# One core's adaLN block: dense column products, two detours through PSUM, and a new order of all operations

## The chip, the cores and the metric

The kernel runs on one NeuronCore of one Trainium2 chip. A core has five engines that run side by side, each through its own queue in order: TensorE (PE, matrix products; its weight loads are shown as PEld), VectorE (DVE), ScalarE (ACT), GpSimd (POOL) and SyncE (SP), which here only issues DMA transfers. Products are written to PSUM, eight banks of 2 KB in each of 128 partitions; everything else lies in SBUF. [...] The metric is device microseconds of one execution.

## What is computed

A transformer block on x of 2048 rows and 512 columns, all in fp32. Six modulation vectors come from one condition vector c. The first half is a linear attention with 32 heads of 16, the second a gated MLP that mixes over the rows:

```python
mod = (silu(c) @ w_mod).reshape(c.shape[0], 6, 1, -1)
sa, ca, ga, sb, cb, gb = (mod[:, k] for k in range(6))
h = layernorm(x) * (1 + ca) + sa
x = x + ga * A(h, wqkv, wo)
h = layernorm(x) * (1 + cb) + sb
x = x + gb * B(h, w_in, w_sp, b_sp, w_out)

# A: linear attention
phi = lambda t: where(t > 0, t + 1, exp(t)) + 1e-6
pq, pk = phi(q), phi(k)
kv  = einsum("bhsd,bhse->bhde", pk, v);  z = einsum("bhsd->bhd", pk)
num = einsum("bhqd,bhde->bhqe", pq, kv)
den = einsum("bhqd,bhd->bhq", pq, z)[..., None] + 1e-6
out = (num / den) merged over heads, @ wo

# B: gated MLP over rows
z = gelu(x @ w_in);  z1, z2 = halves;  z2 = layernorm(z2)
g = einsum("ts,bsf->btf", w_sp, z2) + b_sp[None, :, None]
out = einsum("bsf,fd->bsd", z1 * g, w_out)
```

## The kernel before

The 2048 rows are 16 tiles of 128, numbered t. Nearly every product is done in three passes on pairs of rounded and remaining parts (`mm3`, L108): hi x hi, hi x lo, lo x hi. Each operand is therefore split first: ACT makes the rounded part, DVE or POOL the difference.

The work runs in these stages.

*Start.* The column products `col_mm` (L191) multiply w_mod's second block with silu(c) and give 1 + ca as one column per 128 features. Its weights are 128x128 pieces of w_mod, the moving operand is one column of `sil`, the output one PSUM column. `col_end` (L206) copies the four columns to SBUF. `mean_col` (L325) spreads each of them over 128 columns, four ACT operations from the constant tile `inv` (all 1/512). `mean_mm` (L330) multiplies that with the raw key and query weights to get the mean over features of the scaled weights; `w_mid` (L336) then folds scale and mean into the weights, and `w_hi`, `w_lo` split them. Between the column products stand dummy products (`dummy`, L172; "du" in the order), whose results are not used.

*Projections and moments.* For each tile the x tile is loaded twice, once already transposed (`load_xt`). `k_mm` and `q_mm` give keys and queries in two PSUM banks in turn ("pso"). `phi_in` or `phi_raw` with `phi_add` scale and shift them. `phi_exp` (L438) then makes relu(-t + tiny) and its exponential on ACT, both in one SBUF tile, and `phi_end` (L443) adds max(t, tiny) to it on DVE. `g_mm` accumulates the moments of phi(k) with the normalised x over all 16 tiles.

*Second stage.* The moments are multiplied with the value weights and with wo; the queries are divided by their denominators (`den1`, `den2`), transposed by DMA, and multiplied (`wo_mm`); `x1_out` adds to x, stores it and takes its statistics; `h2` calls `ln_apply` (L259), two DVE operations that scale and shift, both in one SBUF tile; the result is transposed by DMA, split, and multiplied with w_in (`z_mm`), and gelu and the layer norm of its second half follow.

*Row mixing and output* (from ORDER3 on). The first four row tiles of w_sp times z2 are done plainly ("pp"), the rest by a two-by-two scheme with seven products ("pr"). The result is multiplied by z1, transposed by DMA, split and multiplied with w_out ("wm").

Order. Nothing is scheduled by the framework. Two strings, ORDER (from ORDER on, run by `run_all`) and ORDER3, list every operation by a two-letter name and its arguments; each engine receives its instructions in that order. Relevant names: "cm" column product, "ce" col_end, "mc" mean_col, "mr" mean_mm, "wf"/"qh"/"qd"/"qg" fold and split the weights, "kk", "km", "qm" key and query products, "k2"/"q2" phi_exp, "k4"/"q4" phi_end, "h2", "g1"/"g2" gelu of z's two halves, "l5" the load of the sixth modulation block, "lk", "ly", "lw", "lm", "lx" loads. SLOTS lists for each pool which of its buffers every new tile takes, in the order of the list; a tile must wait until the last user of its buffer is done. PSUM's pool "t" (`ps("t", ...)`, "pst") has two banks; the column products, mean products, biases, broadcasts and PE's transposes take them, 17 times in all. Loads and stores are all issued by SP.

Of the kernel before, what the change touches and what calls it, by code (L numbers as in the profile page):

```python
# [26 lines left out]
def block_kernel(ctx: ExitStack, tc: tile.TileContext, x, x_t, w_qkv, w_o, w_in, w_sp, b_sp, w_out,  # L27
# [163 lines left out]
    def col_mm(m, kc):  # L191
        if m not in CP:
            CP[m] = ps("t", [P, KC], f"pcol{m}")
        for i in range(KC):
# [1 line left out]
            mm(CP[m][:, i:i + 1], RAW["mod", m, kc // 2][:, kc % 2, i * P:(i + 1) * P], sil[:, kc:kc + 1],
               start=n == 1, stop=n == KC * KC, skip_group_check=True)
# [61 lines left out]
    def ln_apply(key, src, scale, shift, name):  # L259
        h = sb("ta", [P, D], F32, name)  # L260
        nc.vector.scalar_tensor_tensor(h, src, MEAN[key], scale, op0=OP.subtract, op1=OP.mult)  # L261
# [906 lines left out]
```

## Time and profile before

| | us |
|---|---|
| median of 3 runs | 656.33 (650.57 to 656.46) |
| the profiled execution | 656.31 |
| its span, from first to last instruction | 654.2 |
| bytes moved | 105.74 MB, mean 162 GB/s |

The page gives busy times of each engine over the span, a table in 40 slices, the chain of work that ended last, and groups of instructions by line and shape. Matmuls are pipelined and their ends are modelled, so PE's busy time overstates how densely it works; the distance between the starts of products is the finer measure. A line such as L444 is a line of the kernel; a tile name stands for all tiles of that name with their numbers left out. The rows on which the argument rests are shown in the prediction.

### The profile page before, as it was taken

The page shows a single profiled execution, that of the slowest core. Times are in us where ns is not written, and L with a number is a line of the kernel's source. Part 1 is how long each engine was busy: PE and PEld are TensorE (multiplying, and loading weights), DVE is VectorE, ACT ScalarE, POOL GpSimd, SP SyncE. Part 2 cuts the span into 40 slices and gives each one's busy share as a digit, 9 for nine tenths or more (in the row PEclk, how much of TensorE's full clock was granted, in tenths as well). Part 3 has the DMA queues.
Part 4 walks back from the last instruction along what each step waited for, and adds up shares of the span by engine and source line. Part 5 has one row for each costly group of instructions (what it writes and reads, how often), then busy time and mean ns, then how long its engine had stood idle before and what let it go on. Part 6 is the DMA issues. An engine that isn't in the chain of part 4 may idle for free.

```text
span 654.2 us, 9565 instructions
## 1 busy us (share of the span) xinstructions
PE 629.8 (96%) x3407; PEld 568.7 (87%) x3407; DVE 506.2 (77%) x910; ACT 334.6 (51%) x563; POOL 226.6 (35%) x186
## 2 busy tenths in 40 slices
PE   9999989999889899979999999999999999999998
PEld 9587777777778889879899999999999999998886
DVE  0789999998779689864884579799698789884762
ACT  1577775646446865457452564445444345443430
POOL 0562425625674566633524521140312221110000
PEclk9999999999999999989999999999999999999999
DMA  8235431344234555863473586642745767689862
GB/s 285 105 111 176 129 96 34 113 124 142 61 110 121 116 135 143 199 156 100 142 228 124 174 314 235 150 146 85 215 99 169 209 173 223 173 314 251 261 233 89
DMA packets 91310, 105.74 MB, mean 162 GB/s; under 512 B 57120, under 2 KB 57632, under 8 KB 91264
## 3 DMA queue, kind: packets, MB, share of 16 engines
q1 hardware_dynamic: 91264, 105.15, 53.5%
q8 instruction: 26, 0.43, 0.3%
q14 instruction: 20, 0.16, 0.1%
HBM read 66.07 MB, written 25.95 MB: 141 GB/s over the span
## 4 chain that ended last, share of the span: by engine, by line
PE 44%; DVE 15%; ACT 7%; issue 4%; DMA 3%; POOL 2%; SPq 0%; DVEq 0%; ACTq 0%; POOLq 0%
PE P L930 18%; PE Pq L930 9%; PE z L652 3%; PE pout L111 3%; PE pout L112 3%; PE pout L110 3%; DVE xpp L279 2%; DVE bst L250 2%; DVE xph L279 1%; POOL mv L255 1%; DVE h L262 1%; DMA wor<-in_w_out 1%; DVE ht L299 1%; DVE xr L628 1%; DVE h L261 1%
## 5 line engine op out<-in xcount | busy, mean ns | idle before, releaser
L652 PE MATMUL z<-win,ht 128*128 128x344 f32 x768 | 126.8, 324 | 7.3 <-DVE ht L299 2.8
L652 PEld LDWEIGHTS z<-win,ht 128*128 128x128 f32 x768 | 122.5, 191 | 11.4 <-DVE ht L299 3.5
L930 PE MATMUL P<-z,f 128*128 128x344 f32 x576 | 95.4, 320 | 1.1 <-DVE f L920 1.0
L930 PEld LDWEIGHTS P<-z,f 128*128 128x128 f32 x576 | 91.3, 188 | 1.7 <-DVE f L920 1.6
L920 POOL TENSOR_TENSOR f<-raw_wsp,f 128x512 fp32r<-128x512 f32 x24 | 37.5, 1575 | 122.9 <-ACT f L917 98.6
L255 POOL TENSOR_TENSOR mv<-ve,mhalf 128x1 f32<-128x1 f32 x48 | 37.5, 798 | 74.5 <-DVE ve L254 57.6
L930 PE MATMUL Pq<-z,wsp 128*128 128x344 f32 x384 | 61.5, 321 | 1.3 <-ACT mod L241 1.3
L930 PEld LDWEIGHTS Pq<-z,wsp 128*128 128x128 f32 x384 | 61.0, 188 | 1.6 <-ACT mod L241 1.5
L917 ACT ACTIVATE f<-sa 128x512 fp32r<-128x512 f32 x36 | 22.7, 630 | 50.2 <-DVE sa L907 12.5
L917 ACT ACTIVATE f<-raw_wsp 128x512 fp32r<-128x512 f32 x48 | 29.1, 625 | 21.4 <-PE P L930 9.4
L688 POOL TENSOR_TENSOR z<-zz,z 128x688 fp32r<-128x688 f32 x16 | 29.1, 1834 | 26.0 <-ACT z L685 26.0
L920 DVE TENSOR_TENSOR f<-sa,f 128x512 fp32r<-128x512 f32 x36 | 27.2, 758 | 9.1 <-ACT f L917 9.0
L111 PE MATMUL pout<-wout,ut 128*128 128x512 f32 (+1 forms) x85 | 32.5, 382 | 0.3 <-DVE wout L1050 0.3
L112 PE MATMUL pout<-wout,ut 128*128 128x512 f32 (+1 forms) x85 | 32.3, 380 | 0.0
L110 PE MATMUL pout<-wout,ut 128*128 128x512 f32 (+1 forms) x85 | 32.2, 379 | 0.0
L269 ACT COPY uca<-us 128x768 uint16<-128x768 uint16 x32 | 25.0, 828 | 13.8 <-DVE us L985 10.3
L472 POOL TENSOR_TENSOR pksum<-pksum,tk 128x512 f32<-128x512 f32 x15 | 22.7, 1511 | 26.3 <-DVE tk L444 19.5
L110 PE MATMUL kp<-wk,ht 128*128 128x512 f32 x64 | 26.0, 407 | 3.2 <-DVE tk L423 3.2
L1019 ACT ACTIVATE ut<-ur 128x384 fp32r<-128x384 f32 x32 | 15.5, 519 | 26.4 <-DMA ur<-ud 11.5
L269 ACT COPY xph<-h 128x512 uint16<-128x512 uint16 x28 | 15.9, 615 | 22.4 <-DVE h L262 17.8
L111 PE MATMUL kp<-wk,ht 128*128 128x512 f32 x64 | 25.4, 397 | 1.0 <-DVE wk L345 1.0
L112 PE MATMUL po<-m,pt 128*128 128x512 f32 x64 | 25.3, 396 | 0.6 <-POOL pt L299 0.6
(257 smaller groups left out, 1553.6 us busy)
## 6 DMA issues: line engine op xcount, KB each, us to landing
raw_wsp<-in_w_sp SPq DMA_DIRECT2D x32, 512.0 KB, 5.0
ud<-uca SPq DMA_DIRECT2D x16, 384.0 KB, 3.7
ur<-ud SPq DMA_DIRECT2D x16, 384.0 KB, 4.9
z1d<-z SPq DMA_DIRECT2D x16, 344.0 KB, 2.4
zd<-zz SPq DMA_DIRECT2D x16, 344.0 KB, 2.8
z1r<-z1d SPq DMA_DIRECT2D x16, 344.0 KB, 3.7
xt<-in_x_t SPq DMA_DIRECT2D x16, 256.0 KB, 2.8
x<-in_x SPq DMA_DIRECT2D x16, 256.0 KB, 2.8
```

What stands on the lines that cost most here:

```text
L110: mm(o, a_hi, b_hi, start=first, stop=False, **kw)
L111: mm(o, a_hi, b_lo, start=False, stop=False, **kw)
L112: mm(o, a_lo, b_hi, start=False, stop=last, **kw)
L255: nc.gpsimd.tensor_tensor(mv[:, 1:2], ve, mhalf, op=OP.pow)
L269: nc.scalar.copy(pl[:, h], v[:, :, h])
L279: copy(o[:, :, h], plt[:, h * n:(h + 1) * n].rearrange("p a b -> p (a b)"))
L472: nc.gpsimd.tensor_add(pksum, pksum, PK[t])
L652: mm(p[:, b, :HB], a[:, i, kc], win[h][:, j, kc, b * HB:(b + 1) * HB], start=kc == 0 and k == 0, stop=kc == KC - 1 and k == 2)
L688: nc.gpsimd.tensor_sub(Z2[t][:, 1], ZZ[t], f(Z2[t][:, 0]))
L917: nc.scalar.activation(SF[p, h, k][:, 0], s_src(p, h, k), AF.Copy)
L920: eng.tensor_sub(SF[p, h, k][:, 1], s_src(p, h, k), f(SF[p, h, k][:, 0]))
L930: mm(B[key][:, :HB], a[:, x_], b[:, y_], start=i == 1, stop=i == n)
```

## The change

1. `col_mm` writes 128 equal columns for each feature block: the moving operand is silu(c)'s column broadcast to 128 columns, the output a whole PSUM bank of 4 x 128 columns. `col_end` reads the first column of each block for this key.
2. `mean_col` becomes one ACT operation from that bank, (p + 1)/512, which no longer needs `col_end` or `inv`; the tile `inv` and its fill go.
3. `ln_apply` puts the first of its two results into a PSUM bank of pool "t" and reads it from there.
4. `phi_exp` keeps only the relu; the exponential moves into `phi_end` and writes to a PSUM bank of pool "t", from which DVE's sum reads. Pool "t" is now taken 65 times.
5. ORDER and ORDER3 list the operations in a new order, and SLOTS has new buffers to fit. Six of eleven dummy groups are left out of ORDER: four stand before the first column product and one before the first mean product. The operations of ORDER3 are the same as before, in another order.

```diff
-        "md": "0312013210121201201020120122021201020",
+        "md": "032130213313212312213212313231321312",
...
-        "pst": "01010101010110101",
+        "pst": "01010101010101010101010101010101010101010101010101010101010101010",
...
-    inv = sb("md", [P, P], F32R, "inv")
-    nc.gpsimd.memset(f(inv), 1.0 / D)
...
     def col_mm(m, kc):
         if m not in CP:
-            CP[m] = ps("t", [P, KC], f"pcol{m}")
+            CP[m] = ps("t", [P, KC, P], f"pcol{m}")
         for i in range(KC):
             n = NCOL[m] = NCOL.get(m, 0) + 1
-            mm(CP[m][:, i:i + 1], RAW["mod", m, kc // 2][:, kc % 2, i * P:(i + 1) * P], sil[:, kc:kc + 1],
-               start=n == 1, stop=n == KC * KC, skip_group_check=True)
+            mm(CP[m][:, i], RAW["mod", m, kc // 2][:, kc % 2, i * P:(i + 1) * P],
+               sil[:, kc:kc + 1].to_broadcast([P, P]), start=n == 1, stop=n == KC * KC, skip_group_check=True)
...
     def col_end(key):
         COL[key] = const.tile([P, KC], F32, name=f"col{key}")
-        nc.scalar.activation(COL[key], CP[key], AF.Copy, bias=1.0 if key == 1 else 0.0)
+        p = CP[key][:, :, 0] if key == 1 else CP[key]
+        nc.scalar.activation(COL[key], p, AF.Copy, bias=1.0 if key == 1 else 0.0)
...
     def ln_apply(key, src, scale, shift, name):
         h = sb("ta", [P, D], F32, name)
-        nc.vector.scalar_tensor_tensor(h, src, MEAN[key], scale, op0=OP.subtract, op1=OP.mult)
-        nc.vector.scalar_tensor_tensor(h, h, RSTD[key], shift, op0=OP.mult, op1=OP.add)
+        p = ps("t", [P, D], "p" + name)
+        nc.vector.scalar_tensor_tensor(p, src, MEAN[key], scale, op0=OP.subtract, op1=OP.mult)
+        nc.vector.scalar_tensor_tensor(h, p, RSTD[key], shift, op0=OP.mult, op1=OP.add)
         return h
...
-    def mean_col(kc):
-        if "c" not in WC:
-            WC["c"] = sb("tb", [P, KC, P], F32, "cbr")
-        nc.scalar.activation(WC["c"][:, kc], f(inv), AF.Copy, scale=COL[1][:, kc:kc + 1])
+    def mean_col():
+        WC["c"] = sb("tb", [P, KC, P], F32, "cbr")
+        nc.scalar.activation(WC["c"], CP[1], AF.Copy, scale=1.0 / D, bias=1.0 / D)
...
     def phi_exp(key):
         EK[key] = sb("tb", [P, D], F32, f"e{key[0]}{key[1]}")
         nc.scalar.activation(EK[key], TK[key], AF.Relu, scale=-1.0, bias=tiny)
-        nc.scalar.activation(EK[key], EK[key], AF.Exp, scale=-1.0)
 
     def phi_end(key, o):
-        nc.vector.scalar_tensor_tensor(o, TK.pop(key), TINY, EK.pop(key), op0=OP.max, op1=OP.add)
+        p = ps("t", [P, D], f"p{key[0]}{key[1]}")
+        nc.scalar.activation(p, EK.pop(key), AF.Exp, scale=-1.0)
+        nc.vector.scalar_tensor_tensor(o, TK.pop(key), TINY, p, op0=OP.max, op1=OP.add)
...
     ORDER = """
-        lm1,0 si du1 du2 du3 du4 du5 cm1,0 lm1,1 du6 cm1,1 lm1,2 du7 cm1,2 lm1,3 lk1 lk0 du8 cm1,3 ce1 mc0 ly1
-        mc1 mc3 mc2 lk2 th1 tl1 ly0 th0 tl0 du9 mr1,0 mr1,1 mr1,2 lk3 mr1,3 wf1,3 qh1,3 wf1,1 qh1,1 lw0,0
-        mr0,0 mr0,1 lm0,1 lw0,1 mr0,2 mr0,3 qg1,3 wf1,0 qh1,0 wf1,2 qh1,2 lm0,0 yp0,0 qd1,0 lx0 qg1,1 qd1,2
-        kk0,0 du10 du11 kk0,1 kk1,0 kk0,2 yp0,1 kk0,3 lm0,3 yp0,3 kk1,1 kk1,2 wf0,1 wf0,3 lm0,2 yp0,2 ly2
...
+        lm1,0 lm1,1 si du1 du2 du3 du4 cm1,0 cm1,1 lm1,2 cm1,2 lm1,3 cm1,3 mc lk0 ly1 th1 tl1 lk1 lk2 ly0 th0
+        tl0 lk3 du5 mr1,0 mr1,1 mr1,2 mr1,3 ce1 wf1,3 lw0,0 mr0,0 mr0,1 qh1,3 qg1,3 lw0,1 mr0,2 wf1,0 qh1,0
+        wf1,1 qh1,1 qg1,1 wf1,2 qh1,2 qd1,0 qd1,2 lm0,1 yp0,1 lm0,3 mr0,3 wf0,3 lm0,0 yp0,0 ya0,1 kk1,0 lm0,2
+        yp0,2 ya0,2 wf0,1 yp0,3 ya0,3 wf0,2 wf0,0 ly5 th5 lx0 qh0,1 s10 kk0,0 qh0,3 kk0,1 kk1,1 kk1,2 kk1,3
...
```

More of the change, by code (lines that the diff above doesn't have):

```diff
@@ L810, in block_kernel @@
-        bh15 mS3 bh14 bl14 gm11 bl15 gm12 gm13 qm13 q113 zs zr d12 d13 mB3 d22 vb mB4 wl0,1 d10 d14 gm14 gm15
-        gh0 gh1 li at2 gh2 mk gh3 d11 d23 kv0 l5 lW0,3 wh1,0 d20 kv1 lW0,2 wh0,2 kv2 kv3 kx wh0,3 qm15 wl0,3
-        qm14 d21 wl1,0 q115 lX4 at0 ae0 ae2 mm0 wh1,2 mm1 d17 me0 me1 mm2 me2 mm3 lW1,1 d15 me3 q114 lX0 at3
-        ae3 wh1,1 wl1,1 lW1,3 wl0,2 at1 ae1 wo0 x10 wo3 d24 wo1 x13 w02 h20 ht0 wl1,2 w12 ap4 q213 lX1 d25 he0
-        z00 wh1,3 wl1,3 x12 ap5 am4 ah4 al4 za0 zb0 wo4 h22 hp2 h23 d27 lX11 hp3 am5 ah5 al5 wo5 g10 g20 x11
@@ L815, in block_kernel @@
-        hm2 h21 hh2 hl2 hm3 d16 q413 q214 zl0 ap7 d18 d110 hh3 q414 lX8 ht1 he1 zn0 zp0 d26 z12 g22 zl2 q215
-        z01 lX6 g11 hl3 x14 h24 d19 ap6 hp4 d210 z02 g12 am7 x15 am6 hm4 hh4 h25 z13 g23 ap10 zn2 z11 d112 hl4
-        z04 hp5 z14 q415 d115 d28 g21 ah7 al7 wo7 d29 ah6 al6 g14 zl1 zh2 zl3 d111 d215 hm5 lX7 g24 ap9 am10
-        hh5 wo6 hl5 z15 x17 ap8 zp2 d211 h27 am9 hp7 d212 ah10 g25 al10 zl4 am8 ah8 al8 z03 g13 zn4 zh0 zo0
-        lX10 ah9 zo2 hm7 lX9 z05 hh7 g15 ap11 wo10 wo8 x16 ap12 zl5 hl7 z17 d113 h26 hp6 al9 wo9 x110 lX14 zp4
@@ new lines, in block_kernel @@
+        me2 d14 at3 lW1,3 wh1,3 mm1 me1 at1 q114 mm3 me3 wo0 ae3 wo3 d15 wh1,0 lX4 wl1,0 w02 d24 lW1,1 wh1,1
+        lX0 x10 ae1 wo1 q214 d17 ap4 x13 wl1,1 h20 ht0 d25 he0 w12 za0 z00 wl1,3 x12 zb0 ap5 am4 ah4 al4 wo4
+        q213 h22 hp2 d27 h23 q413 hp3 q215 am5 ah5 al5 wo5 lX9 hm2 lX5 x11 h21 ht1 hh2 hl2 z12 ap7 hm3 g10 x14
+        g20 zl0 he1 q414 hh3 hl3 q415 d115 g22 zn0 z01 g11 x15 h24 hp4 z02 d16 d111 d26 z13 h25 hp5 g12 hm4
+        hh4 ap6 g23 l5 d18 d19 d28 lX8 hl4 hm5 hh5 am7 ah7 al7 z11 g21 zh0 zo0 lX7 hl5 lX6 zl2 z04 d211 z14
@@ new lines, in block_kernel @@
+        g14 am6 ah6 ap8 d110 z03 d29 wo7 g24 zp0 d210 zn2 d215 ap10 zp2 zl4 ap9 al6 x17 d112 g13 zn4 zp4 h27
+        zh2 z15 hp7 z05 am10 ah10 wo6 al10 d113 am8 ah8 am9 wo10 al8 wo8 ap11 d212 zl3 x16 ah9 ap12 al9 wo9
+        h26 hp6 x110 hm7 hh7 x18 hl7 g15 h28 z07 g25 z17 lX12 hp8 am11 ah11 al11 wo11 hm6 hh6 d213 x19 hm8 hh8
+        hl6 z16 hl8 z08 g27 lX11 am12 ah12 g17 h29 hp9 al12 wo12 zh4 zo4 x111 ap13 h211 zn3 zp3 hm9 zl5 h210
+        hh9 hl9 zl7 g18 zo2 d114 hp11 hp10 zh3 g26 zl6 zn5 zp5 lX15 d214 z19 g29 z06 g16 hm10 hh10 ap14 z09
@@ L828, in block_kernel @@
+        zl11 zn11 zh11 zo9 z115 g114 zp11 mB5 aL0,0 aL1,0 g215
     """
@@ L1132, in block_kernel @@
+        wm3 uh4 ot1 ul4 ur6 uh6 um14 up14 ur10 ug12 uq12 uq13 ul6 ur7 ux14 lx14 lz15 wm4 uh5 wm2 ot2 uh8 ur9
+        ul5 ug14 uq14 lx11 uh7 lx6 wm6 ul7 lx10 ot3 ur12 uh10 ur13 ul8 wm5 uh12 wm8 cd7,4 um15 up15 wm7 ot4
+        ot5 ur11 ur14 ul10 uh9 lx13 ul9 ot6 ux15 ot7 ot8 uh14 ul14 wm10 ul12 wm9 wm12 ug15 uq15 uh11 ul11 wm11
+        ot9 ot10 uh13 ul13 wm13 ur15 uh15 wm14 ot11 ot12 ul15 wm15,0,256 ot13 ot14 ot15,0,256 wm15,256,512
+        ot15,256,512
     """
```

162 lines of the change are left out of this document (78 added, 84 removed).

## The prediction

> **What bounds the kernel now.** I read the page's head first, then the table by stages, then who PE waits for, and then the first 28 us line by line.
>
> ```profile
> span 654.2 us, 9565 instructions
> ...
> PE 629.8 (96%) x3407; PEld 568.7 (87%) x3407; DVE 506.2 (77%) x910; ACT 334.6 (51%) x563; POOL 226.6 (35%) x186
> ```
>
> PE is busy for 96% of the span, so only three things can be had: PE work that need not be done, PE work at a low clock, and the 24.4 us in which PE stands idle.
>
> ```profile
> core 0: us, PE busy (x) PEld busy (x) DVE busy (x) ACT busy (x) POOL busy (x), PEclk, DMA share, GB/s
> 0.00:24.40 24.40, 23.41 (x84) 18.44 (x85) 4.58 (x10) 5.92 (x13) 1.93 (x10) 1.00 0.72 258
> 24.40:130.00 105.60, 102.70 (x445) 81.49 (x444) 100.70 (x171) 74.78 (x122) 52.56 (x42) 1.00 0.33 103
> 130.00:300.00 170.00, 156.01 (x825) 137.00 (x824) 138.39 (x254) 96.97 (x164) 93.39 (x80) 0.99 0.48 126
> 300.00:360.00 60.00, 59.12 (x350) 55.98 (x349) 39.05 (x71) 30.98 (x48) 24.00 (x19) 1.00 0.53 162
> 360.00:587.00 227.00, 224.69 (x1421) 223.65 (x1420) 186.35 (x327) 106.98 (x185) 54.76 (x38) 1.00 0.62 191
> 587.00:655.00 68.00, 63.83 (x292) 52.14 (x290) 37.13 (x81) 18.99 (x36) 0.00 (x0) 1.00 0.68 208
> ```
>
> The stages differ. In the start (to 24.4) PE is busy with 84 instructions, few for its time. From 24.4 to 130 (keys, queries, moments) PE idles 2.9 us, but DVE is busy for 100.7 of 105.6: both are full, and whichever starts late sets the end. From 130 to 300 nothing is full and PE idles 14.0 us, more than half of all its idle time: chains of short waits between engines. From 300 on PE is all but full, and no order of the work can give much there: 0.9 and 2.3 us up to 587, and the last window runs past the end of the span.
>
> ```profile
> PE kp L110 <- DVE tk L423: 3.2, 2, 1.6
> PE pm L110 <- DVE m L130: 2.9, 1, 2.9
> PE z L652 <- DVE ht L299: 2.8, 2, 2.3
> PE z L652 <- ACT zz L663: 2.1, 2, 1.1
> ```
>
> The longest single waits of PE are 1.6 to 2.9 us, most of them for DVE and ACT results of the second stage; no one of them is worth 1%.
>
> **The start, step by step.** These are rows of the timeline, all engines; the weight loads (PEld) tell the spacing of the products.
>
> ```profile
> 0.99 4.64 PE L174 MATMUL warm<-ones 128*128 128x128 f32 x20 [0.99 <-POOL ones L120]
> ...
> 5.42 1.71 PE L196 MATMUL pcol<-sil,raw_mod 128*128 128x1 f32 x8
> 6.31 0.33 SPq L156 DMA_DIRECT2D raw_qkv<-in_w_qkv  x1
> ...
> 9.75 0.33 SPq L144 DMA_DIRECT2D raw_qkv<-in_w_qkv  x1
> ...
> 15.11 1.28 ACT L328 ACTIVATE cbr<-inv,col 128x128 f32<-128x128 f32 x4
> ...
> 15.66 9.33 PE L334 MATMUL wm<-raw_qkv,cbr 128*128 128x512 f32 x16
> ...
> 16.58 0.34 PEld L334 LDWEIGHTS wm<-raw_qkv,cbr 128*128 128x128 f32 x1 [0.52 <-ACT cbr L328]
> ...
> 17.43 0.34 PEld L334 LDWEIGHTS wm<-raw_qkv,cbr 128*128 128x128 f32 x1 [0.52 <-issue]
> ...
> 20.53 0.19 PEld L334 LDWEIGHTS wm<-raw_qkv,cbr 128*128 128x128 f32 x1 [0.24 <-issue]
> 20.96 0.19 PEld L334 LDWEIGHTS wm<-raw_qkv,cbr 128*128 128x128 f32 x1 [0.24 <-PE wm L334]
> ...
> 21.59 2.72 DVE L338 SCALAR_TENSOR_TENSOR wf<-raw_qkv,col,wm 128x512 f32<-128x512 f32 x4 [3.36 <-PE wm L334]
> ...
> 24.42 0.79 PE L110 MATMUL kp<-wk,ht 128*128 128x512 f32 x1
> ...
> 26.77 1.05 PE L174 MATMUL warm<-ones 128*128 128x128 f32 x8
> ```
>
> The mean products (L334) start 0.85 us apart (16.58, 17.43) and later 0.43 us apart (20.53, 20.96); a load takes 0.34 and then 0.19. So PE runs at half speed until about 20 us, although it had work without a gap from 0.99 on. The column PEclk says 1.00 there, so the spacing is the better witness. The dummy products tell the same: 4.64/20 = 0.23 us each at first, 1.05/8 = 0.13 after 26.77. Half speed lasts until products of 512 columns have run for some 4 us; the products of one column (L196, 0.21 us each) did not raise it.
>
> ```profile
> raw_qkv<-in_w_qkv SPq DMA_DIRECT2D x4, 512.0 KB, 5.9
> ...
> raw_qkv<-in_w_qkv SPq DMA_DIRECT2D x4, 256.0 KB, 6.8
> ```
>
> **The change at the start.** (a) The column products become 128 columns wide. At half speed they cost what they do now: the 128-column dummies of L174 take 0.23, the one-column products 0.21. (b) Of the five dummy groups that stand from just before the first of them to the mean products one stays, behind the last; each holds 4 products, about 0.9 us at half speed. (c) The four ACT operations of L328 (1.28 us) give way to one that reads PSUM, about 0.59 by the row of L241 below, and the small column copy leaves the path. The new chain: four dummies to 0.99 + 16 x 0.23 = 4.7; 32 products of 0.21 to 11.5 at half speed, or about 9 if the clock rises on the way; one dummy group and the column operation beside each other, about 0.6. Then the data decide: the last 256 KB part of the key weights is issued at 6.31 and lands 6.8 later, at 13.1, and its place in the load order is unchanged (two others swap). So the key half of the mean products ends at 13.1 + 2 x 0.43 = 14.0 at full speed. The second half of the query weights (9.75 + 5.9 = 15.7, one place earlier now) gives 15.7 + 4 x 0.43 = 17.4 for the rest. DVE starts on the folded weights at 14.1 instead of 21.59, 7.5 us earlier; the first key product stands at about 18 instead of 24.42. Behind it two more dummy groups (26.77, 1.05 us) go. PE would gain 6.4 to 7.5, and DVE, the other full engine of the next stage, 7.5. I take **7.4**; bounds 4.2 (the clock rises no earlier than the mean products, worked out below) and 9.1 (the waits between 24.42 and 26.77 go too).
>
> [...]
>
> **The two detours through PSUM.** Rows by shape, with busy time and mean ns:
>
> ```profile
> L262 DVE SCALAR_TENSOR_TENSOR h<-h,mv,mod 128x512 f32<-128x512 f32 x16 | 15.6, 976 | 3.9 <-POOL mv L255 3.1
> ...
> L261 DVE SCALAR_TENSOR_TENSOR h<-xr,mv,mod 128x512 f32<-128x512 f32 x16 | 14.2, 888 | 0.0
> ...
> L444 DVE SCALAR_TENSOR_TENSOR tk<-tk,ek 128x512 f32<-128x512 f32 x16 | 13.0, 811 | 1.8 <-ACT ek L441 1.8
> ...
> L444 DVE SCALAR_TENSOR_TENSOR pq<-tq,eq 128x512 f32<-128x512 f32 x14 | 11.2, 812 | 2.4 <-ACT eq L441 2.0 <-issue 0.3
> ...
> L423 DVE SCALAR_TENSOR_TENSOR tq<-qp,mv,kqb 128x512 f32<-128x512 f32 x14 | 10.2, 735 | 0.9 <-ACT kqb L380 0.9
> L441 ACT ACTIVATE ek<-ek 128x512 f32<-128x512 f32 x16 | 10.1, 634 | 0.5
> ...
> L241 ACT ACTIVATE mod<-pmod 128x512 f32<-128x512 f32 x4 | 2.4, 588 | 0.0
> ...
> L444 DVE SCALAR_TENSOR_TENSOR pq<-pq,eq 128x512 f32<-128x512 f32 x2 | 1.4, 678 | 0.0
> ```
>
> The same operation takes 678 ns in its best form and 811 or 976 elsewhere, all tensors in SBUF; with one input from PSUM (L423) it takes 735. So phi's sum goes from 811 to about 735, 32 x 0.076 = 2.4 us, nearly all in the stage where DVE is full: **2.0** on the path. The second half of the scaling goes from 976 to 735, 16 x 0.24 = 3.9 us in a stage where DVE has room; the chain of waits below gives L262 1% of the span, 6.5 of its 15.6 us, so four tenths count: **1.6**. A write by DVE to PSUM isn't in the trace: the first half (888) lies between 678 and 976 either way, and I cost it at nothing, since its two inputs stay in SBUF. A write by ACT to PSUM isn't in it either: 588 (a read from PSUM) to 634, and I leave it at 634.
>
> [...]
>
> The exponential also moves behind, to just ahead of the sum, so the last ones fall together: counted in the two orders, ACT changes between exponential and gelu tables five times now and three times then. The five of now, first and last of them here, lie between 206 and 224, among PE's waits for ACT's gelu. Two loads of 1.28 go; half counts: **1.3**.
>
> ```profile
> 205.94 1.28 ACT L657 ACT_TABLE_LOAD   x1
> ...
> 222.78 1.28 ACT L657 ACT_TABLE_LOAD   x1
> ```
>
> ```profile
> PE P L930 18%; PE Pq L930 9%; PE z L652 3%; PE pout L111 3%; PE pout L112 3%; PE pout L110 3%; DVE xpp L279 2%; DVE bst L250 2%; DVE xph L279 1%; POOL mv L255 1%; DVE h L262 1%; DMA wor<-in_w_out 1%; DVE ht L299 1%; DVE xr L628 1%; DVE h L261 1%
> ```
>
> **What it adds.** The two rotating PSUM banks of the "t" pool, taken 17 times now, are taken 65 times: 32 by phi, 16 by the scaling. ACT's exponential then waits until DVE has finished the sum two turns back, and behind it in ACT's queue stand the splits that feed PE. The broadcasts, column parts and transposes on PE take the same banks. Cost: nothing while ACT is at least one sum ahead (it is busy 71% in that stage, 74.78 of 105.6), up to 0.63 each when not; I take 0.06 x 32 = **2.0**, near the 1.8 + 2.4 us that DVE waits for L441 today. The new order of everything else: SP's loads keep their places but for a few (query weights before the modulation, the sixth modulation's loads later), and the DMA share of 0.33 to 0.68 after the start leaves room; POOL (35% busy) loses a fill. From 300 on PE is the bound in either order. Between 130 and 300 the new order can win or lose part of the 14.0 us: I take nothing, bounds -8 and +6.
>
> Sum: -7.4 - 2.0 - 1.6 - 1.3 + 2.0 = -10.3. The profiled execution took 656.3 with a span of 654.2, 2.1 around it, and the median of the runs is the same 656.3. So 643.9 + 2.1 = **646.0**.
>
> **The rivals.**
> - The second stage also comes out better, with half of its 14.0 us of waits gone: about 639. For it: many small waits, none of them forced. Against: nothing in the change aims at them but the shorter sums.
> - The clock does not rise early (the change doesn't do what it says). Column products to 11.5, 0.9 of dummies, then 8 key products at 0.85 to 19.2 and 8 more at 0.43 to 22.6: first key product 1.8 earlier, with the 1.05 and about 1.3 of waits behind it 4.2 in place of 7.4: 649.2.
> - The start is won and given back: the next stage is as full on DVE as on PE, and small waits of the new order (+6 between 130 and 300) eat it: 652.
> - Slower: phi's sum waits for its own exponential. The exponential now comes just before the sum, may start only when a bank is free, and if ACT is no longer ahead, DVE, full in that stage, stands for 0.634 at each of 32: +20.3 in place of 2.0, so 646.0 + 18.3 = 664. It decides (over 1% slower) from 0.59 each on. Against: ACT has a quarter of that stage free.
>
> **How the numbers follow.** My forecast 0.48 (own range 641 to 651); better second stage 0.13; clock late 0.12; given back 0.15; slower 0.12. About 1% is what a measurement here can tell from no change: below 649.8 is faster, above 662.9 slower. Faster: 0.48 + 0.13, without a tail of the forecast that passes 649.8, and half of the late clock: 0.62. Slower 0.12, the rest 0.26. The range 637 to 657 leaves out the slower case and the tails, 0.2 in all.
>
> **What would show it.** Right: L334 spaced 0.43 from its first product, the first key product near 18, L444 near 0.74 and L262 near 0.74, four table loads. Wrong: L334 still 0.85 apart; DVE idle before L444 for the new exponential by much over 4 us; PE's idle time between the end of the start and the gelu stage well over 17 us.

## The result and the profile after

| | us |
|---|---|
| before, median of 4 runs beside the next | 654.33 (650.57 to 656.46) |
| after, median of 4 runs | 629.19 (628.49 to 629.97) |
| after / before | 0.962, 95% interval 0.957 to 0.968 |
| after: span of the profiled execution | 628.2 (before 654.2) |

The forecast was 646.0 with a range of 637 to 657. The kernel became faster, as said, but by about 25 us and not by 10; the time lies below the range.

The head of the page after, and the table by stages, cut at the same places in the work as the table of before (first key product, middle of the projections, middle of the gelu stage, first row-mixing product, first output product):

```profile
span 628.2 us, 9510 instructions
...
PE 617.6 (98%) x3383; PEld 562.8 (90%) x3383; DVE 475.0 (76%) x910; ACT 331.6 (53%) x558; POOL 216.6 (34%) x185
```

```profile
0.00:17.30 17.30, 15.79 (x67) 10.82 (x68) 5.11 (x10) 5.76 (x10) 2.17 (x9) 1.00 0.81 291
17.30:120.00 102.70, 102.23 (x445) 82.73 (x444) 93.68 (x176) 74.51 (x123) 51.52 (x44) 1.00 0.39 126
120.00:280.00 160.00, 157.40 (x842) 141.54 (x841) 125.08 (x251) 93.97 (x161) 90.43 (x77) 0.98 0.50 132
280.00:338.00 58.00, 58.00 (x353) 56.35 (x351) 36.85 (x83) 32.81 (x49) 24.77 (x21) 1.00 0.60 177
338.00:562.00 224.00, 220.99 (x1395) 219.49 (x1394) 177.60 (x314) 107.79 (x184) 47.72 (x35) 1.00 0.64 189
```

PE's idle time in the second and third row is 0.5 and 2.6 us; in before the like rows had 2.9 and 14.0. DVE, with the same 910 instructions, is busy 31.2 us less. Who PE waits for between 17 and 338 us:

```profile
PE pkv L721 <- DVE gh L128: 1.6, 1, 1.6
PE tpp L306 <- POOL pq L593: 0.7, 1, 0.7
PE kp L110 <- ACT tk L432: 0.5, 1, 0.5
```

The waits for `tk` (L423), `m`, `ht` and gelu's results that headed the list of before are gone. The start, as the rows of the timeline show it:

```profile
4.68 4.41 PE L194 MATMUL pcol<-sil,raw_mod 128*128 128x128 f32 x32
...
9.12 0.60 ACT L327 ACTIVATE cbr<-pcol 128x512 f32<-128x512 f32 x1 [6.51 <-PE pcol L194]
9.77 0.30 PEld L333 LDWEIGHTS wm<-raw_qkv,cbr 128*128 128x128 f32 x2 [0.43 <-ACT cbr L327]
...
14.08 2.72 DVE L337 SCALAR_TENSOR_TENSOR wf<-raw_qkv,col,wm 128x512 f32<-128x512 f32 x4 [0.55 <-PE wm L333]
...
14.73 0.19 PEld L333 LDWEIGHTS wm<-raw_qkv,cbr 128*128 128x128 f32 x1 [0.24 <-issue]
15.16 0.19 PEld L333 LDWEIGHTS wm<-raw_qkv,cbr 128*128 128x128 f32 x1 [0.24 <-issue]
...
17.33 0.80 PE L110 MATMUL kp<-wk,ht 128*128 128x512 f32 x1
```

The mean products stand 0.43 us apart (14.73, 15.16), and where they stand wider they wait for loads (2.5 us in all until a part of `raw_qkv` has landed), not for the clock. DVE starts on the folded weights at 14.08 (forecast 14.1), the first key product at 17.33 (forecast about 18).

For the experiments it helps to cut the span at four marks that every trace shows: the first key product, the end of the score sums (`g`), the first `z` product, the first row-mixing product (`Pq`). All numbers are from the profiled executions. "Drawn out" is worked out from the trace between 24 and 340 us: for each group of DVE operations of one form, the time of each above the time that the fastest fifth stays under, summed. "Median" and "ratio" are of the timed runs, each against before on the same chip.

| kernel | first key product | to end of scores | to first z | to first Pq | drawn out | median | ratio to before, 95% |
|---|---|---|---|---|---|---|---|
| before | 24.4 | 141.1 | 30.1 | 169.1 | 41.0 | 654.3 | |
| after | 17.3 | 133.3 | 31.9 | 156.5 | 13.5 | 629.2 | 0.957 to 0.968 |
| a_narrow | 19.3 | 133.8 | 32.0 | 156.5 | 13.6 | 632.1 | 0.965 to 0.975 |
| a_dummies | 17.9 | 133.8 | 29.0 | 156.5 | 14.9 | 630.6 | 0.959 to 0.967 |
| a_nd | 24.4 | 133.8 | 32.0 | 156.5 | 15.7 | 636.8 | 0.965 to 0.977 |
| b_start | 17.8 | 140.3 | 31.4 | 169.1 | 40.9 | 650.6 | 0.990 to 0.997 |
| as_both | 17.4 | 136.2 | 29.1 | 159.2 | 28.6 | 630.3 | 0.962 to 0.972 |
| as_phi | 16.9 | 135.8 | 29.0 | 156.6 | 21.8 | 628.3 | 0.959 to 0.967 |
| as_h | 17.4 | 133.4 | 30.6 | 159.5 | 20.6 | 630.3 | 0.963 to 0.970 |
| b_h | 24.6 | 141.1 | 30.0 | 165.0 | 35.6 | 651.8 | 0.991 to 0.998 |
| h_bb | 17.6 | 140.3 | 31.7 | 166.4 | 37.2 | 651.6 | 0.992 to 0.998 |
| h_ab | 16.6 | 133.3 | 35.4 | 174.5 | 23.7 | 664.2 | 1.009 to 1.019 |
| b_nopool | 20.9 | 135.2 | 31.2 | 158.2 | 2.7 | 636.4 | 0.968 to 0.976 |
| a_nopool | 17.0 | 133.1 | 26.2 | 156.0 | 4.1 | 622.2 | 0.946 to 0.954 |
| a_again | 17.3 | 133.3 | 30.5 | 156.5 | 13.5 | 629.5 | 0.958 to 0.966 |
| a_bz | 16.3 | 133.8 | 26.2 | 156.5 | 12.4 | 625.4 | 0.952 to 0.959 |
| b_bz | 24.5 | 141.1 | 29.6 | 169.4 | 38.8 | 654.3 | 0.997 to 1.002 |

So between before and after the start gave 7.1 us, the projections 7.8, the gelu stage 12.6; the middle (from the end of the scores to the first `z` product) took 1.8 more, and everything behind the first `Pq` product is unchanged (0.3).

Some of these numbers hold a piece of luck. Behind the start, each trace has a few stretches, or none, in which PEclk is 0.50 instead of 1.00; they last 3.4 or 6.8 us, but for those that the end of the trace cuts off. Before has one of 3.4 in its gelu stage, at 290 us, and none in the middle; after has one of 6.8 in the middle and none in the gelu stage. Eight kernels, after among them, have the same stall of PE in the middle, 1.60 us: with no half clock behind it the middle takes 29.0 or 29.1 us (a_dummies, as_both, as_phi), with 3.4 us 30.5 or 30.6 (a_again, as_h), with 6.8 us 31.9 or 32.0 (after, a_narrow, a_nd). A stretch thus cost the middle about half its length (1.5 of 3.4 us, 2.9 of 6.8): by that estimate 1.7 us of the gelu stage's 12.6 are before's stretch.

### The profile page after: what moved, and what is told of

Its sections match the earlier page's. It is cut to its first block, busy times and chain, and to the rows that moved or that the text cites. A ratio compares the mean times of both kernels' runs of the same rounds, so it can differ in the third digit from the quotient of the medians.

```text
span 628.2 us, 9510 instructions
## 1 busy us (share of the span) xinstructions
PE 617.6 (98%) x3383; PEld 562.8 (90%) x3383; DVE 475.0 (76%) x910; ACT 331.6 (53%) x558; POOL 216.6 (34%) x185
## 4 chain that ended last, share of the span: by engine, by line
PE 54%; DVE 7%; DMA 4%; ACT 2%; issue 1%; POOL 1%; SPq 0%; DVEq 0%; ACTq 0%; POOLq 0%
PE z L652 18%; PE P L930 18%; PE Pq L930 4%; PE pout L111 3%; PE pout L112 3%; PE pout L110 3%; PE po L112 2%; DMA o<-zd 2%; DMA raw_wsp<-in_w_sp 2%; PE po L110 2%; PE po L111 2%; DVE f L920 1%; PE pout L1068 1%; PE pout L1067 1%; ACT zz L675 1%
## 5 line engine op out<-in xcount | busy, mean ns | idle before, releaser
L652 PE MATMUL z<-win,ht 128*128 128x344 f32 x768 | 122.3, 320 | 0.0
L920 POOL TENSOR_TENSOR f<-raw_wsp,f 128x512 fp32r<-128x512 f32 x24 | 34.2, 1435 | 122.1 <-ACT f L917 105.2
L254 POOL TENSOR_TENSOR mv<-ve,mhalf 128x1 f32<-128x1 f32 x48 | 36.8, 770 | 74.3 <-DVE ve L253 38.8
L917 ACT ACTIVATE f<-raw_wsp 128x512 fp32r<-128x512 f32 x48 | 30.0, 629 | 37.6 <-PE P L930 16.3
L688 POOL TENSOR_TENSOR z<-zz,z 128x688 fp32r<-128x688 f32 x16 | 27.6, 1728 | 19.5 <-ACT z L685 19.5
L110 PE MATMUL kp<-wk,ht 128*128 128x512 f32 x64 | 25.8, 403 | 0.5 <-ACT tk L432 0.5
L472 POOL TENSOR_TENSOR pksum<-pksum,tk 128x512 f32<-128x512 f32 x15 | 20.9, 1395 | 13.9 <-DVE tk L444 11.5
L112 PE MATMUL kp<-wk,ht 128*128 128x512 f32 x64 | 25.3, 395 | 0.0
L111 PE MATMUL kp<-wk,ht 128*128 128x512 f32 x64 | 25.3, 395 | 0.0
```

Of the source, the lines that this page charges most:

```text
L110: mm(o, a_hi, b_hi, start=first, stop=False, **kw)
L111: mm(o, a_hi, b_lo, start=False, stop=False, **kw)
L112: mm(o, a_lo, b_hi, start=False, stop=last, **kw)
L254: nc.gpsimd.tensor_tensor(mv[:, 1:2], ve, mhalf, op=OP.pow)
L472: nc.gpsimd.tensor_add(pksum, pksum, PK[t])
L652: mm(p[:, b, :HB], a[:, i, kc], win[h][:, j, kc, b * HB:(b + 1) * HB], start=kc == 0 and k == 0, stop=kc == KC - 1 and k == 2)
```

## Why VectorE's operations were long

Before the experiments, a part of before's trace that the prediction did not use. Here are DVE and POOL side by side at two of PE's waits, the 1.65 us for `tk` at 91 us and the 2.30 us for `ht` at 287 us (rows of the timeline: start, duration, engine, line, operation; other engines' rows are left out):

```profile
89.46 1.38 POOL L472 TENSOR_TENSOR pksum<-pksum,tk 128x512 f32<-128x512 f32 x1
89.60 1.78 DVE L404 TENSOR_TENSOR ht<-xt,ht 128x512 fp32r<-128x512 f32 x1
91.31 0.74 DVE L396 SCALAR_TENSOR_TENSOR hhl<-x,mv,hhl 128x512 fp32r<-128x512 f32 x1
91.97 0.74 DVE L423 SCALAR_TENSOR_TENSOR tk<-kp,mv,kqb 128x512 f32<-128x512 f32 x1
...
284.89 1.47 POOL L299 TENSOR_TENSOR pt<-xpp,pt 128x512 fp32r<-128x512 f32 x1
285.14 1.77 DVE L261 SCALAR_TENSOR_TENSOR h<-xr,mv,mod 128x512 f32<-128x512 f32 x1
287.01 0.75 DVE L262 SCALAR_TENSOR_TENSOR h<-h,mv,mod 128x512 f32<-128x512 f32 x1
287.35 1.91 POOL L688 TENSOR_TENSOR z<-zz,z 128x688 fp32r<-128x688 f32 x1 [0.99 <-ACT z L685]
287.68 2.13 DVE L299 TENSOR_TENSOR ht<-xph,ht 128x512 fp32r<-128x512 f32 x1
...
289.86 0.66 PE L652 MATMUL z<-win,ht 128*128 128x344 f32 x1 [2.30 <-DVE ht L299]
```

The subtractions `ht` take 0.68 us in the median of the trace and 1.78 and 2.13 here. In all three pairs a POOL operation had begun just before, and the DVE operation ends 0.54 to 0.55 us after it: 89.46 + 1.38 = 90.84 and 89.60 + 1.78 = 91.38; 284.89 + 1.47 = 286.36 and 286.91; 287.35 + 1.91 = 289.26 and 289.81. By these ends DVE stood still until POOL was done. Over the whole span DVE's operations are drawn out by some 65 us in before and 32 in after (where the fastest fifth is cut off moves such a sum by about 1 us). The difference is DVE's whole saving of 31.2. In before 64 operations take over 0.15 us longer than the fastest fifth of their group; while each of them runs, a POOL operation ends, and in 63 of the 64 POOL's had begun first.

Which operations were struck is as clear: those with two tensors from SBUF (`hhl` up to 1.79, `h` 1.86 and 2.17, phi's sum 1.78, `ht` 2.13, all with medians of 0.68 to 0.75), and copies from SBUF to SBUF (`xph` up to 1.94, median 0.46). Of the 12 + 14 + 16 operations that take one tensor from PSUM (`tk` from `kp`, `tq` from `qp`, `xr` with `po`) none takes over 0.75.

So theory C (collision): PE waited where a DVE operation on its path had met a POOL operation; the new order, and by a smaller part the detours, freed PE of those meetings. Rival Q (queue): the operations stood in the wrong place in DVE's queue, however long they take. Rival D (detours): the gain is the detours'.

## The experiments

**The detours taken off PSUM.** phi's exponential and the scaling's first half write to two SBUF buffers in turn, so that order and waits stay (to make room, the buffers of `tb` are cut from 768 to 688 columns, and some small tiles get one buffer each).

```diff
+    def st(name):
+        s = slot("pst")
+        return pst_sb.tile([P, D], F32, tag="x" + s, name=name)
...
-        p = ps("t", [P, D], "p" + name)
+        p = st("p" + name)
...
-        p = ps("t", [P, D], f"p{key[0]}{key[1]}")
+        p = st(f"p{key[0]}{key[1]}")
```

as_both has both, as_phi the second line alone, as_h the first.

> The kernel after, with both detours taken off the PSUM banks: phi's exponential and the first half of the scaling write to two buffers in SBUF that take turns just as the banks did; order, waits and operation counts stay. Theory A (the extra gain of 17 us behind the start comes from the new order, the detours only shorten VectorE, which is not what ends the stages): 631 to 634 us, the second key/query stage and the gelu stage no more than 3 us longer between their milestones, the products' idle time as in after. Theory B (the detours carry it, since they take 31 us off VectorE and VectorE's lateness was what the products waited for): 640 to 646 us, with the end of the score sums near 156 us instead of 150.6 and the end of the gelu stage near 350 instead of 337.9. In both theories the scaling goes back from 741 and 751 ns to about 888 and 976, the phi sums from 680 to about 810.

> The kernel after with phi's exponential alone written to SBUF. Theory A: 630 to 632 us (32 phi sums x 0.13 us = 4 us more of VectorE, nearly all beside other work). Theory B: 635 to 638, the loss between the first key product and the end of the score sums (about 6 us).

> The kernel after with the first half of the second scaling alone written to SBUF. Theory A: 630 to 632 us (16 x 0.37 us = 6 us more of VectorE, mostly beside products). Theory B: 638 to 643, the loss between 182 and 338 us (about 13 us).

As a whole, theory A: 630.3, 628.3 and 630.3 against 629.2. By stages the detours do work: without phi's the projections take 2.5 us longer, without the scaling's the gelu stage 3.0 (the third and fifth column of the table; both sets of stages add up in as_both). But the middle then takes 1.3 to 2.9 less and the part behind the first `Pq` 1.8 to 2.9 less, so that little of it shows at the end. The first is the luck of the half clock (0 to 3.4 us of it here, 6.8 in after), the second goes with a wait of 1.79 us of a `Pq` product at 379 us that after has and these three don't; no run shows whether the detours have a part in that. DVE in as_both:

```profile
L270 DVE SCALAR_TENSOR_TENSOR h<-ph,mv,mod 128x512 f32<-128x512 f32 x16 | 17.8, 1115 | 5.8 <-POOL mv L262 4.8 <-DVE ph L269 0.5
...
L452 DVE SCALAR_TENSOR_TENSOR tk<-tk,pk 128x512 f32<-128x512 f32 x16 | 13.2, 834 | 3.4 <-ACT pk L451 3.4
```

In after the same rows read:

```profile
L444 DVE SCALAR_TENSOR_TENSOR tk<-tk,pk 128x512 f32<-128x512 f32 x16 | 10.8, 681 | 4.0 <-ACT pk L443 4.0
...
L262 DVE SCALAR_TENSOR_TENSOR h<-ph,mv,mod 128x512 f32<-128x512 f32 x16 | 12.0, 751 | 5.7 <-POOL mv L254 4.7 <-DVE ph L261 0.5
```

With `p` in SBUF the second half takes 1115 ns on average, with `p` in PSUM 751, which is its undisturbed time. Rival D is out for the 17 us behind the start. Nor does drawn-out time by itself tell the gain: from b_start to as_both (order and moved exponential) it falls from 40.9 to 28.6 us and the time by 20.3; from as_both to after (the detours) it falls by more, to 13.5, and the time by 1.1.

**The start alone, and one detour alone, in before's order.**

```diff
-            CP[m] = ps("t", [P, KC], f"pcol{m}")
+            CP[m] = ps("t", [P, KC, P], f"pcol{m}")
...
-        lm1,0 si du1 du2 du3 du4 du5 cm1,0 lm1,1 du6 cm1,1 lm1,2 du7 cm1,2 lm1,3 lk1 lk0 du8 cm1,3 ce1 mc0 ly1
+        lm1,0 si du1 du2 du3 du4 cm1,0 lm1,1 cm1,1 lm1,2 cm1,2 lm1,3 lk0 lk1 cm1,3 mc ly1
```

> The kernel before with the start alone changed: dense column products, one mean-column operation instead of four, no reciprocal tile, the six dummy groups left out; every later operation in before's order, no detours. If the start's gain is its own and is kept (the prediction's sum): first key product near 17.5 us instead of 24.4, 644 to 647 us. If it is given back because later stages wait for loads and for VectorE anyway: first key product early, but the end of the score sums still near 165 us, 650 to 654. If the start's gain needs the new order: first key product at 20 us or later.

The start comes 6.6 us earlier, and in the old order it is kept: first `z` product 6.1 earlier, last output product 5.0 (646.2 against 651.2), median 4.4. The projections take 140.3 and the gelu stage 169.1, as in before. Nothing else moved but the middle, 1.3 longer with 3.4 us at half clock in it.

> The kernel before with the first half of the second scaling through the PSUM banks, and nothing else. If VectorE's length set the waits of the gelu stage under the old order (8 of its 14 us of waits name VectorE's results): the 16 x 0.37 us that it is relieved of give 3 to 6 us, 646 to 649 us. If the waits came from where the operations stand in VectorE's queue, and not from their length: 650 to 653 us, the waits of the z products still there.

(The edit is that of `ln_apply` in the change.) The gelu stage is 4.1 us shorter, of which 1.7 is before's stretch at half clock, which b_h's profiled execution doesn't have. The time is about 3 shorter (0.991 to 0.998); 651.8 is short of the 646 to 649 that were expected if VectorE's length set the waits. In the old order this detour shortened waits of PE, by 1.7 us in that stage: the 976 ns of L262 were 751 plus meetings. The first half, which still takes two tensors from SBUF though it writes to PSUM, is drawn out up to 2.18 us here. Writing to PSUM did not save the first half from its meetings; of the 16 second halves that read from PSUM in after, none took over 0.75.

**Which half of the order.** h_ab is after up to the last score sums and before's order from there on; the list is after's up to `gm15` and then holds what is left in before's order. h_bb is before's order throughout, with the new start and the scaling's detour but with phi as in before. In both, the buffers behind the score sums were given out anew, and both have before's ORDER3.

```diff
-        q113 d13 gm14 gm15 lX2 lW0,3 wh0,3 wl0,3 wh0,2 d10 qm15 d22 lX1 d23 gh0 gh2 li at2 gh1 q115 kv0 kv1 mk
-        kv2 gh3 kv3 ae2 d11 wh0,1 wl0,1 d20 kx qm14 lW1,2 wh1,2 wl1,2 mB3 d21 wl0,2 lW1,0 mm0 me0 at0 ae0 mm2
...
+        ks14 ks15 zx mS4 bl14 kh15 kl15 zs zr d12 mB4 lW0,2 bh15 bl15 cv vb q113 d13 gm14 gm15 lX2 wh0,1 lX5 lW1,2
+        lW1,0 mB3 d22 wl0,1 d10 d14 gh0 gh1 li at2 gh2 mk gh3 d11 d23 kv0 l5 lW0,3 wh1,0 d20 kv1 wh0,2 kv2 kv3 kx
...
```

> Before's order throughout, with the start changed as in b_start and the second scaling's first half in PSUM, and the buffers behind the score sums given out anew (a control for the next kernel). Order theory: within 3 us of b_start, 643 to 649 us, end of the score sums near 158, first z product near 188, end of the gelu stage near 356. Detour theory's remainder: 637 to 641, the gelu stage 8 us shorter than in b_start.

> The kernel after up to the last score sums, then the remaining operations in before's order, with buffers given out as in the control. Order theory, the gain split by stage: the projections as in after (end of the score sums near 151), the gelu stage as long as before's (169 us from the first z product to its end, against 155 in after), 638 to 643 us. If the gelu stage's gain comes from what the projections leave behind (buffers and loads ready earlier), and not from its own order: the gelu stage near 157 us, 630 to 633.

The new projections keep their gain under the splice (133.3). The gelu stage does not: 174.5, longer than in any other kernel. But the splice has waits of its own, and three stretches of 3.4 us at half clock behind them in the gelu stage; between 24 and 365 us PE waited

```profile
PE z L645 <- ACT zz L656: 6.4, 3, 3.1
PE pm L103 <- DVE m L121: 2.9, 1, 2.9
PE tpp L299 <- POOL pq L586: 2.5, 1, 2.5
```

and the 6.4 us are gelus that stand behind exponentials and their table loads, which the change puts with phi's sum and which before's list has in the midst of the gelus (at 225.64 and 229.23 us the trace has the two loads of 1.28). So h_ab shows that the gelu stage's gain does not come with the projections' part of the new order, and that the moved exponential costs time in an order that wasn't made for it; it is no price of before's order. For that h_bb stands (166.4, with the detour). Behind the first `Pq` the two also lose 6.5 and 12.2 us against before, where buffers given out anew meet ORDER3; the stages ahead of it are what they were run for.

**GpSimd's reads taken away.**

```diff
-        nc.gpsimd.tensor_sub(Z2[t][:, 1], ZZ[t], f(Z2[t][:, 0]))
+        nc.gpsimd.memset(f(Z2[t][:, 1]), 0.0)
+        nc.gpsimd.tensor_sub(Z2[t][:, 1, 0:1], ZZ[t][:, 0:1], f(Z2[t][:, 0, 0:1]))
...
-            nc.gpsimd.tensor_add(pksum, pksum, PK[t])
+            nc.gpsimd.tensor_add(pksum[:, 0:1], pksum[:, 0:1], PK[t][:, 0:1])
```

> The kernel before, with GpSimd's work up to the end of the gelu stage cut: sums, products and low parts there are done on one column only, and where the rest would be left unwritten it is set to zero first by an operation that only writes; so the sums, the denominators and the low parts are not the reference's. Order, queues and waits stay. Collision theory (the products waited behind VectorE operations that had been drawn out from 0.7 to 1.8 us while GpSimd read SBUF; the new order avoids those meetings): VectorE's drawn-out time goes from 65 us to under 25, the score sums end 5 to 7 us earlier counted from the first key product, the gelu stage takes 156 to 160 us instead of 169, 636 to 642 us in all. Queue theory (VectorE's operations stand in the wrong place, whatever they take): both stages within 2 us of before, 650 to 654 us.

> The kernel after with the same cut of GpSimd's work. Collision theory: little is left to win, since the new order has already moved the meetings to where no product waits: 626 to 629 us. Queue theory: 628 to 630, as in after. If GpSimd itself limits after in some place: under 625.

This is the run that decides between C and Q. In before's own order, with every VectorE operation in its old place, the projections take 135.2 instead of 141.1 and the gelu stage 158.2 instead of 169.1 (1.7 of it before's half clock), within 2 us of after. DVE's rows in b_nopool:

```profile
L262 DVE SCALAR_TENSOR_TENSOR h<-h,mv,mod 128x512 f32<-128x512 f32 x16 | 12.0, 752 | 3.6 <-POOL mv L255 2.6
L396 DVE SCALAR_TENSOR_TENSOR hhl<-x,mv,hhl 128x512 fp32r<-128x512 f32 x16 | 11.9, 747 | 0.1
...
L299 DVE TENSOR_TENSOR ht<-xph,ht 128x512 fp32r<-128x512 f32 x14 | 9.6, 688 | 9.9 <-ACT ht L295 9.8
```

976, 1036 and 878 ns have become 752, 747 and 688, with all tensors in SBUF. What PE still waits for is what does not hang on a meeting:

```profile
PE pm L110 <- DVE m L130: 2.9, 1, 2.9
PE z L655 <- ACT z L660: 1.7, 2, 1.1
PE pkv L725 <- DVE gh L130: 1.0, 1, 1.0
```

The 2.9 us for `m` are as in before; that one is a matter of order (in after transposes stand between these products on PE, and the wait is gone). GpSimd's own results come sooner as well in this run; but PE had waited for them only 0.6 us in before, and the waits of DVE and ACT for them, 4.3 and 4.6 us between 24 and 345 us, are 5.7 and 4.1 here. The start is 3.5 us earlier in this execution (20.9), which is not the cut's doing (see the last experiment); the stages are counted from there.

In after the same cut gains 7 us, more than the collision theory had put down (626 to 629), and nearly all of it in one place: the middle, 26.2 instead of 31.9.

**One meeting at a time.** That place is the stall in front of the key/value products at 154 us. Of its rows in after:

```profile
146.40 4.41 DVE L712 TENSOR_SCALAR bz<-zrep,colv 128x128 f32<-128x128 f32 x4
147.59 1.68 POOL L532 TENSOR_TENSOR win<-raw_win,win 128x688 fp32r<-128x688 f32 x1
149.21 1.31 POOL L581 TENSOR_TENSOR prod<-pq,zrep 128x512 f32<-128x512 f32 x1
...
153.38 0.32 ACT L590 ACTIVATE den<-den,tiny 128x32 f32<-128x32 f32 x1 [0.97 <-DVE den L589]
153.61 1.06 ACT L127 ACTIVATE gh<-g 128x512 fp32r<-128x512 f32 x2
...
156.32 0.58 PE L721 MATMUL pkv<-gh,wv 128*128 128x256 f32 x1 [1.60 <-DVE gh L128]
```

Four small bias products (`bz`) take 4.41 us while POOL reads; behind them in DVE's queue stand the denominators, behind those in ACT's queue the first part of the score sums, and behind that PE. After the stall the clock drops:

```profile
150.00:155.80 5.80, 4.06 (x19) 2.86 (x17) 4.83 (x10) 2.47 (x6) 3.15 (x4) 1.00 0.22 61
155.80:162.60 6.80, 6.28 (x29) 6.28 (x30) 3.26 (x6) 1.81 (x4) 3.43 (x3) 0.50 0.31 90
```

The summed keys that `bz` reads still lie in a PSUM bank, so one word takes the meeting away:

```diff
-            nc.vector.tensor_scalar(KV["b"][:, g, :], KV["z"][:, g * P:(g + 1) * P], COL["v"][:, g:g + 1], None,
+            nc.vector.tensor_scalar(KV["b"][:, g, :], KV["p"][:, g * P:(g + 1) * P], COL["v"][:, g:g + 1], None,
```

> The kernel after, unchanged, beside the next one on the same chip. Both theories: 628 to 631 us, a stall of some 1.8 us ahead of the key/value products and half clock behind it.

> The kernel after, its four bias products reading the summed keys from the PSUM bank they were summed in, instead of the copy in SBUF. Collision theory: the four take 0.6 to 1.2 us together instead of 4.4, the denominators and with them ScalarE's halves of the scores' sums come 3 us earlier, the 1.8 us stall and the half clock behind it are gone: 3 to 5 us faster than after, 624 to 627 us. Rival (the stall comes from the chain of the last scores' sums itself, whatever stands ahead of it): the four shorter, the stall still there, 628 to 631 us.

> The kernel before with the same edit. Collision theory: the four take about 0.8 us instead of 3.0, the 1.6 us stall ahead of the key/value products shrinks to under 1 us (its operands come from the score sums, which end just there), so 0.5 to 1.6 us faster between the end of the score sums and the first z product; in the whole time that is lost in before's own spread of 8 us. Rival: the stall stays at 1.6 us.

In a_bz, the rows at the same place:

```profile
145.84 1.11 DVE L712 TENSOR_SCALAR bz<-pz,colv 128x128 f32<-128x128 f32 x4
...
149.76 1.07 ACT L127 ACTIVATE gh<-g 128x512 fp32r<-128x512 f32 x2
```

```profile
150.00:155.80 5.80, 5.80 (x41) 5.24 (x40) 4.76 (x8) 3.61 (x7) 4.41 (x4) 1.00 0.15 53
155.80:162.60 6.80, 6.80 (x38) 5.37 (x37) 4.66 (x8) 3.21 (x7) 3.60 (x4) 1.00 0.28 90
```

4.41 us become 1.11, `gh` comes 3.85 us earlier (0.56 of it was won ahead of the four), the stall and the half clock are gone, and the middle takes 26.2 us as with all reads cut. The stall and the half clock are two things. In as_both the same stall ends at 159.3 us, and the clock stays full:

```profile
155.80:162.60 6.80, 4.55 (x35) 3.87 (x34) 5.70 (x11) 3.96 (x8) 5.02 (x4) 1.00 0.00 0
162.60:170.00 7.40, 7.31 (x38) 5.61 (x38) 5.35 (x9) 4.24 (x8) 4.13 (x4) 1.00 0.33 93
```

So the stall costs the middle 2.8 us (29.0 in as_phi against 26.2), and the half clock up to 2.9 more, as the execution has it. The four runs lie between 623.5 and 626.3, those of after beside them between 627.8 and 631.8: 4.2 us faster in the median, the fastest version that computes everything. It takes 3.3 us off DVE and gains 4.2, because PE stood behind these operations, and in part because of the clock: its mean is 1.000 in the profiled execution, the fastest of the four, and 0.997 in the other three, against 0.992 to 0.997 in after's. The start, 1.0 earlier than after's in the profiled execution, is not the edit's doing. phi's detour takes 8.3 us of drawn-out time away (as_phi 21.8, after 13.5) and the end shows nothing of it. The sum is no price; what counts is whether PE stands behind the operation struck. (The column shows only 1.1 us for `bz`, since three of its four were struck and there is hardly a fastest fifth to measure from.) In b_bz the four shrink too, but the stall only from 1.5 to 1.0 us, since the last score sum, on which the products hang, ends just there: the middle 0.5 shorter, the time the same. Both as theory C had it.

**What made the start fast.**

```diff
-            mm(CP[m][:, i], RAW["mod", m, kc // 2][:, kc % 2, i * P:(i + 1) * P],
-               sil[:, kc:kc + 1].to_broadcast([P, P]), start=n == 1, stop=n == KC * KC, skip_group_check=True)
+            mm(CP[m][:, i, 0:1], RAW["mod", m, kc // 2][:, kc % 2, i * P:(i + 1) * P],
+               sil[:, kc:kc + 1], start=n == 1, stop=n == KC * KC, skip_group_check=True)
...
-        lm1,0 lm1,1 si du1 du2 du3 du4 cm1,0 cm1,1 lm1,2 cm1,2 lm1,3 cm1,3 mc lk0 ly1 th1 tl1 lk1 lk2 ly0 th0
+        lm1,0 lm1,1 si du1 du2 du3 du4 cm1,0 lm1,2 du6 cm1,1 lm1,3 du7 cm1,2 du8 cm1,3 mc lk0 ly1 th1 tl1 lk1 lk2 ly0 th0
```

a_narrow has the first edit (and reads one column for all), a_dummies the second with the other three groups, a_nd both.

> The kernel after with the column products one column wide again, everything else as it is (no dummies put back, same order). Prediction's theory (dense products raise the granted clock early): clock at half until about 20 us, mean products 0.85 apart instead of 0.43, first key product near 22 to 24, 634 to 637 us. Rival (the start was won by leaving out the dummies and by the order of the loads; width does nothing): first key product near 17.3, 628 to 630 us.

> The kernel after with the six groups of dummy products put back where before had them (three between the column products, one ahead of the first mean product, two behind the first key products), column products dense. If the dummies' own time is most of the start's gain: each of the four ahead of the mean products costs 0.5 to 1.2 us, first key product at 19.5 to 21, 631 to 633 us. If the loads set the start anyway: first key product at 17.3 to 18, 629 to 630 us.

> The kernel after with one-column products and the six dummy groups, as before's TensorE had them. If dummies and thin products together keep the clock down (as in before): column products end near 14.8 us, mean products 0.85 apart, first key product at 23 to 24.5, 635 to 637 us. If the dummies hold the clock up for the thin products: first key product at 18 to 20 us, 630 to 633 us.

In the profiled executions each alone costs little: thin products put the first key product at 19.3 (+2.0), the dummies at 17.9 (+0.6). Together they put it at 24.4, exactly before's: +7.1 where the sum of the two is 2.6. What the clock does is seen in a_narrow's first stages, where the column PEclk tells it this time:

```profile
4.90:9.20 4.30, 4.01 (x30) 3.84 (x31) 0.00 (x0) 0.00 (x0) 0.00 (x0) 0.91 0.89 275
9.20:13.00 3.80, 3.80 (x10) 2.25 (x11) 1.14 (x2) 1.80 (x4) 0.00 (x0) 0.50 1.04 411
13.00:17.40 4.40, 4.40 (x9) 1.94 (x8) 1.13 (x3) 0.11 (x1) 0.00 (x0) 0.75 1.04 403
```

With thin products the clock was at half from about 8.4 us on, and the mean products then went 0.85 apart until 15. That hurts little, since the key half of the loads they wait for lands until 12.5 anyway. With the dummies between them at half clock (1.20 us for a group of four, against 0.61 at full) the column products of a_nd end at 14.1 instead of 9.1, the mean products begin at 15.8 instead of 9.8, with all their loads there, and every microsecond counts.

But which clock thin products meet differs from one execution to the next. b_nopool has before's start unchanged, and in the same 4.3 us PE gets through 36 instructions there and 23 in before (the row of before first; ahead of the first change that the trace holds, at 6.1 us in b_nopool and at 20.2 in before, the column PEclk says 1.00 whatever the clock was):

```profile
4.90:9.20 4.30, 4.30 (x23) 4.30 (x22) 0.00 (x0) 0.00 (x0) 0.00 (x0) 1.00 0.87 251
4.90:9.20 4.30, 4.30 (x36) 4.30 (x34) 0.00 (x0) 0.00 (x0) 0.00 (x0) 1.00 0.95 269
```

With this the first key product stands at 20.9 instead of 24.4. The timed runs differ likewise: a_nd's took 634.0 and 634.3, or 639.2 and 640.3, a_narrow's 631.0 to 632.8, or 635.7. So it is not shown that thin products and dummies together cost more than each by itself; with one trace of each, that may be the clock that each met. What does hold in every trace is the width. In the eleven with dense column products all sixteen weight loads of the mean products take 0.19 us; in the six with thin ones the first six or seven take 0.29 to 0.34.

## Why the prediction was right or wrong

- *The start, -7.4:* right in size (the first key product 7.1 earlier, b_start 6.6, of which 4.4 to 6 reached the end) and in its time points (14.1, 18). The reason, that dense products have the clock up before the mean products, holds in all eleven traces that have them (0.19 us for each weight load of the mean products). That the size came out so near is luck in part: before was profiled with a long start (24.4; the same instructions took 20.9 in b_nopool), and in the timed runs b_start is worth 4.4.
- *phi's sums -2.0 and the scaling's second half -1.6:* the ends were right (681 and 751 ns against 735 forecast), the worth in their stages larger (2.5 and 3.0), at the end of after smaller (1.1 for both), and the reason wrong. I read 811 against 735 as a difference between SBUF and PSUM. The medians are 0.68 and 0.75 either way; 811 and 976 were means over undisturbed and struck operations.
- *Two table loads, -1.3:* six became four, as counted; their worth was not measured by itself.
- *Coupling through the banks, +2.0:* DVE idles 5.1 us before L444's sums instead of 4.2, 0.9 more. The rival in which phi's sum waits for its exponential at every tile is out.
- *The order, "I take nothing, bounds -8 and +6":* **this is the step that failed.** b_start to as_both, which differ in the order and in where the exponential stands, is 4.1 us in the projections and 9.9 in the gelu stage (1.7 of it a stretch at half clock that only b_start's has), 12 to 14 us where the sum had nothing, beyond the bound and in part outside the stretch that I bounded: for the projections the sum had no term of the order at all. Two readings led there. "DVE is busy for 100.7 of 105.6: both are full" took DVE's busy time for work, and some 14 us of it was DVE standing behind POOL. And the 14.0 us of PE's waits were taken for chains that an order moves about, though the rows of DVE beside POOL would have shown that those for `tk` and `ht` had a cause that an order can remove. The rival "the second stage also comes out better" came nearest, at 0.13 and at half its size; no rival had the projections' gain.
- *The base:* the forecast was made from an execution of 656.3, and before's runs lie between 650.4 and 658.3 in all, after's within 4. That costs the forecast some 2 us, not 17.

What stays open: what of the 14 us each moved operation brings (only b_bz and a_bz took out single meetings); whether the order gains by fewer meetings or by placing those that are left where PE doesn't stand behind them, as as_both, which keeps 28.6 us of drawn-out time, suggests; and whether the table loads count. Nor is it settled why before's own times spread over 8 us. The clock at the start has a part in it: b_nopool's trace shows 3.5 us from it with before's instructions, and a_nd, with before's start, spreads nearly as much (633.9 to 640.3).
